# A decode block on one core: W2's four loads written behind the fills of the zero tiles instead of ahead of them

## The chip, the core and the metric

The kernel runs on one core of a Trainium2 chip. The metric is the device time of one execution in microseconds; less is better. The core has five engines, each with an instruction stream of its own: TensorE (PE in the profile, its weight loads PEld), VectorE (DVE), ScalarE (ACT), GpSimd (POOL) and SyncE (SP). A transfer is issued by an instruction on one of them and runs on 16 DMA engines.

## The reference

One decode step for two sequences (B = 2, one token each, D = 512) in float32: attention over a cache of 8192 positions with 32 heads of 128, then a channel MLP of width 1792, each with a residual around it.

```
x = A_x
h = x + _A_ref(_layernorm(x), K, V, wq, wo)        # attention
h2 = h + _B_ref(_layernorm(h), w1, b1, w2, b2)     # MLP

_A_ref: q = x @ wq; p = softmax(q K^T * Dh**-0.5); o = p V; return o @ wo
_B_ref: y = layernorm(x); g = gelu(y @ w1 + b1);   return g @ w2 + b2
```

The work is nearly all loading: 562.06 MB are read from HBM, most of it K and V.

## The kernel before

Heads go in pairs, 16 pairs by 2 sequences: 32 units, each with one K tile and one V tile of 128 partitions by 16384 numbers. VectorE multiplies K by q and sums up the scores, with GpSimd adding halves of three chunks in four. ScalarE makes the exponentials. TensorE sums over V in `values(i, t)`: 32 steps u of 512 columns each, in the profile two records a step. Nearly all loads are issued from GpSimd's queue by `soft` (line 437).

All large tiles share one ring of three buffers (`kv` in the profile; `slot()` gives out the oldest). The last to be given out are these. `vlast` is the V tile of the last unit, 31, loaded in four parts of 64, 32, 24 and 8 positions. `wt` holds W1, W2 and the biases, in the buffer that the weights Wo had before. `late` has the buffer of the V tile of unit 30, and `cut()` slices it from column 0 on into the small tiles of the program's end: `zeros` (columns 0 to 95, filled with zero at L700; `otz` and `lane` are its parts, and L703 copies ones into `lane`), then `wlc`, `base` and `basec`, then `wb` (columns 2144 to 2399, filled with zero at L722).

The order on each engine is the order of the code. `Waits` looks at every instruction as it is written and has it wait, by semaphores, for the latest instruction that still uses the same partitions and columns: a fill of `late` waits for those of TensorE's matmuls in `values(30)` that read the columns it covers. GpSimd's loads have semaphores of their own in turn (`soft_0` to `soft_11`).

TensorE's end is in this order: `values` of unit 30; the four parts of the last unit's `values`, with two matmuls of zeros (`keep_warm(FILL[0])`, which read `wb`) written between the second and third part, at u = 24; products with `lane`; `head_sum`; products with `otz`; W1 in two halves, each behind one of W1's two loads; W2 in 14 steps t, behind W2's four loads of 7, 4, 2 and 1 steps. `keep_warm` stands at four other places in between. At L793 VectorE adds the bias, and SyncE stores the result.

```
vlast = load(v, NU - 1, [(0, NS2 // 2), (NS2 // 2, 32), (NS2 // 2 + 32, 24), (NS2 - 8, 8)])
wt = slot()
...
late = slot()
...
zeros = cut(P, (TH + 1) * 32)
nc.gpsimd.memset(zeros, 0.0)
...
        if i == NU - 1 and u == 24:
            keep_warm(FILL[0])
```

Of the kernel before, what the change touches and what calls it, by code (L numbers as in the profile page):

```python
# [273 lines left out]
def tile_decode_block(nc, waits, x, k, v, wq, wo, wog, wol, w1, bias, w2, out):  # L274
    B, H, SK, DH = k.shape
    D = wq.shape[0]
    F = w1.shape[1]
    DC = D // P
    FN = F // NG
    FT = F // P  # L280
# [17 lines left out]
    def slot():  # L298
        return kv.tile([P, ROW], F32, name="kv", tag="kv")
# [136 lines left out]
    def soft(to, of, joined=True):  # L436
        nc.gpsimd.dma_start(to, of, single_packet=joined)  # L437
# [74 lines left out]
    def inverse(g):  # L512
        r = work.tile(list(RL[g].shape), F32, name="rl" if g < GL else "rlp")
        nc.vector.reciprocal(r, RL[g])  # L514
        RL[g] = r
# [159 lines left out]
    wt = slot()  # L675
# [5 lines left out]
    w1v = w1.rearrange("(p c) f -> p c f", c=DC)  # L681
    for c in range(0, DC, 2):
        soft(w1t[:, c:c + 2], w1v[:, c:c + 2])
    w2t = wt[:, DC * F:2 * DC * F].rearrange("p (t d) -> p t d", t=FT)
    w2v = w2.rearrange("(p t) d -> p t d", t=FT)
    for t, n in ((0, 7), (7, 4), (11, 2), (13, 1)):
        soft(w2t[:, t:t + n, :], w2v[:, t:t + n, :])

    inverse(GL)
    nc.scalar.activation(junk[:, 0:1], lt4[:, 0:1], AF.Sqrt)  # L690

# [3 lines left out]
    def cut(parts, n):  # L695
        at[0] += n
        return late[:parts, at[0] - n:at[0]]
# [22 lines left out]
    nc.vector.tensor_scalar(basec, base, bmean, None, op0=ALU.subtract)  # L720
    wb = cut(P, D // 2).bitcast(BF16)
    nc.gpsimd.memset(wb, 0.0)  # L722

    po2 = psq.tile([P, P], F32, name="po2", tag="qps")
    wp = psq.tile([P, D], F32, name="wp", tag="qps", ahead=1)
# [119 lines left out]
```

## Time and profile before

| | us |
|---|---|
| median of 3 runs | 1306.67 (1305.98 to 1308.36) |
| profiled execution | 1308.55 |
| its span | 1306.3 |
| PE busy | 383.8 (29%) |
| DVE busy | 951.4 (73%) |
| ACT busy | 51.7 (4%) |
| POOL busy | 484.0 (37%) |
| DMA, share of the chain of waits | 71% |

The span runs from the first to the last instruction of the profiled execution; its time has 2.25 us more around it. The transfers run at 430 GB/s over the span, with the DMA engines busy in nearly every slice, so the middle of the program is set by loading; the program's end is a chain of small dependent steps behind the last loads. Times in the views are from the span's start. L437 is the line of all loads from GpSimd, so they are told apart by their tensor and size; `in_w_dram` stands for W1 and W2 both. L194 is the helper's line for matmuls outside the loop.

### The profile page before, as it was taken

The page shows a single profiled execution, that of the slowest core. Times are in us where ns is not written, and L with a number is a line of the kernel's source. Part 1 is how long each engine was busy: PE and PEld are TensorE (multiplying, and loading weights), DVE is VectorE, ACT ScalarE, POOL GpSimd, SP SyncE. Part 2 cuts the span into 40 slices and gives each one's busy share as a digit, 9 for nine tenths or more (in the row PEclk, how much of TensorE's full clock was granted, in tenths as well). Part 3 has the DMA queues.
Part 4 walks back from the last instruction along what each step waited for, and adds up shares of the span by engine and source line. Part 5 has one row for each costly group of instructions (what it writes and reads, how often), then busy time and mean ns, then how long its engine had stood idle before and what let it go on. Part 6 is the DMA issues. An engine that isn't in the chain of part 4 may idle for free.

```text
span 1306.3 us, 6773 instructions
## 1 busy us (share of the span) xinstructions
PE 383.8 (29%) x2897; PEld 120.4 (9%) x2900; DVE 951.4 (73%) x411; ACT 51.7 (4%) x172; POOL 484.0 (37%) x215
## 2 busy tenths in 40 slices
PE   4005023230412323043331403333041332403267
PEld 1001000000100001010000101000010100101113
DVE  1988677779777778877778877777986777887742
ACT  0010000000000000000000000000000000000011
POOL 2444433244443234443234443324444323444320
PEclk9557566665666657566665756666566665656678
DMA  9999999999999999999999999999999999999997
GB/s 401 434 448 421 441 426 438 429 436 431 435 432 435 431 437 429 438 429 437 429 437 429 437 429 437 429 437 429 437 428 439 427 439 427 439 428 437 419 429 324
DMA packets 11500, 561.20 MB, mean 430 GB/s; under 512 B 1420, under 2 KB 1428, under 8 KB 1758
## 3 DMA queue, kind: packets, MB, share of 16 engines
q0 software_dynamic: 11168, 552.61, 97.9%
q1 hardware_dynamic: 314, 8.41, 1.6%
q8 instruction: 8, 0.13, 0.0%
q14 instruction: 6, 0.05, 0.0%
q10 hardware_dynamic: 4, 0.00, 0.0%
HBM read 562.06 MB, written 0.00 MB: 430 GB/s over the span
## 4 chain that ended last, share of the span: by engine, by line
DMA 71%; DVE 14%; POOL 11%; PE 2%; issue 2%; ACT 0%; DVEq 0%
DMA kv<-in_k_dram 69%; DVE kv L471 12%; POOL kv L475 10%; DVE s L478 2%; DMA kv<-in_wq_dram 1%; PE so L194 1%; PE qps L194 1%; POOL kv L437 0%; PE sm L194 0%; PE rowacc L194 0%; DVE rl L514 0%; DVE q L407 0%; ACT kv L784 0%; POOL kv L678 0%; POOL kv L722 0%
## 5 line engine op out<-in xcount | busy, mean ns | idle before, releaser
L471 DVE TENSOR_TENSOR kv<-kv,qps 128x4096 f32<-128x4096 f32 x128 | 564.0, 4407 | 277.0 <-DMA kv<-in_k_dram 275.0
L475 POOL TENSOR_TENSOR kv<-kv 128x2048 f32<-128x2048 f32 x96 | 434.1, 4523 | 472.3 <-DVE kv L471 272.0
L478 DVE TENSOR_REDUCE s<-kv 128x32 f32<-128x2048 f32 (+1 forms) x128 | 357.1, 2810 | 0.6 <-POOL kv L475 0.3
L242 PE MATMUL so<-kv,pt 128*16 128x512 f32 x1920 | 272.1, 730 | 270.8 <-DMA kv<-in_v_dram 248.6
L242 PE MATMUL sm<-ident,mx 128*1 128x128 f32 x30 | 9.7, 324 | 571.9 <-DVE mx L485 571.9
L437 POOL DMA_DIRECT2D kv<-in_v_dram x35 | 19.3, 551 | 273.0 <-DVE mx L485 251.7
L242 PEld LDWEIGHTS so<-kv,pt 128*16 128x16 f32 x1920 | 62.0, 112 | 456.0 <-DMA kv<-in_v_dram 250.0
L242 PEld LDWEIGHTS sm<-ident,mx 128*1 128x1 f32 x30 | 2.4, 79 | 578.0 <-DVE mx L485 574.9
L534 ACT ACTIVATE ss<-so 128x512 f32<-128x512 f32 x16 | 9.6, 597 | 551.3 <-PE so L242 514.1
L497 ACT ACTIVATE nb<-sm 128x4 f32<-128x4 f32 x16 | 2.8, 173 | 652.5 <-PE sm L242 649.5
L502 ACT ACTIVATE pt<-s,nb 64x128 f32<-64x128 f32 x64 | 25.5, 399 | 1.7
L437 POOL DMA_DIRECT2D kv<-in_k_dram x33 | 18.8, 570 | 8.7 <-DVE s L478 8.7
L194 PE MATMUL qps<-kv,pt 128*16 128x512 f32 x128 | 17.7, 702 | 8.7 <-DMA kv<-in_v_dram 8.7
L242 PE MATMUL sm<-ss,sel 128*4 128x128 f32 x120 | 15.6, 273 | 12.5 <-ACT ss L534 11.6
L407 DVE COPY q<-so 128x512 f32<-128x512 f32 x1 | 0.7, 691 | 18.3 <-PE so L194 18.3
L514 DVE RECIPROCAL rlp<-sm 128x4 f32<-128x4 f32 x1 | 0.2, 181 | 17.3 <-PE sm L194 17.3
L194 PE MATMUL so<-kv,yT 128*4 128x512 f32 x64 | 10.0, 793 | 8.6 <-DMA kv<-in_wq_dram 8.6
L490 DVE TENSOR_REDUCE gm<-sm 1x4 f32<-1x256 f32 x16 | 6.6, 412 | 7.3 <-PE sm L242 7.0
L242 PEld LDWEIGHTS sm<-ss,sel 128*4 128x4 f32 x120 | 9.3, 87 | 28.2 <-ACT ss L534 17.3
L502 ACT ACTIVATION_READ_ACCUMULATOR pt<-s,nb 64x1 f32 x64 | 11.8, 184 | 0.0
L437 POOL DMA_DIRECT2D kv<-in_w_dram x6 | 3.2, 534 | 22.9 <-issue 22.9
L242 PE MATMUL qps<-qs,pick 4*128 4x128 f32 x60 | 11.1, 306 | 0.0
(122 smaller groups left out, 160.4 us busy)
## 6 DMA issues: line engine op xcount, KB each, us to landing
kv<-in_k_dram POOLq DMA_DIRECT2D x2, 4096.0 KB, 18.3
kv<-in_wq_dram SPq DMA_DIRECT2D x1, 6656.0 KB, 18.3
kv<-in_wo_dram POOLq DMA_DIRECT2D x1, 6144.0 KB, 31.0
kv<-in_w_dram POOLq DMA_DIRECT2D x3, 1792.0 KB, 32.1
kv<-in_v_dram POOLq DMA_DIRECT2D x1, 4096.0 KB, 27.2
kv<-in_v_dram POOLq DMA_DIRECT2D x1, 2048.0 KB, 27.4
kv<-in_wq_dram SPq DMA_DIRECT2D x1, 1536.0 KB, 21.6
kv<-in_v_dram POOLq DMA_DIRECT2D x1, 1536.0 KB, 26.8
```

Source lines behind the costliest of these rows:

```text
L194: getattr(self.nc.tensor, what)(*aps, **how)
L242: ins = getattr(pe, what)(*aps, **how)
L407: nc.vector.tensor_copy(q2, so2[0])
L437: nc.gpsimd.dma_start(to, of, single_packet=joined)
L471: nc.vector.tensor_tensor(kc, kc, QP[g][:, b, None, :].to_broadcast([P, CH, DH]), op=ALU.mult)
L475: nc.gpsimd.tensor_tensor(kc[:, :, 0:HP], kc[:, :, 0:HP], kc[:, :, HP:DH], op=ALU.add)
L478: nc.vector.tensor_reduce(S[i][:, c * CH:(c + 1) * CH], chunk(t, c)[:, :, 0:n], axis=AX.X, op=ALU.add)
L490: nc.vector.tensor_reduce(gm, MT.pop(g).rearrange("o b (s p) -> o b s p", s=2), axis=AX.X, op=ALU.max, negate=True)
L497: nc.scalar.activation(nb, GM.pop(g), AF.Copy)
L502: nc.scalar.activation(ptz[b][q, :, 4 * m:4 * m + 4], s[q], AF.Exp, bias=nb[q, b, e:e + 1], scale=SCALE, accum_out=lt4[q, m:m + 1])
L514: nc.vector.reciprocal(r, RL[g])
L534: nc.scalar.activation(SS[g], so2[g == GL], AF.Copy)
```

## The change

The four loads of W2 are written some 30 lines later: behind the fill of `zeros`, the copy into `lane` and the fill of `wb`. Nothing is added or taken away, and all else stays in its place.

```
--- before.py
+++ after.py
@@ -681,11 +681,6 @@
     w1v = w1.rearrange("(p c) f -> p c f", c=DC)
     for c in range(0, DC, 2):
         soft(w1t[:, c:c + 2], w1v[:, c:c + 2])
-    w2t = wt[:, DC * F:2 * DC * F].rearrange("p (t d) -> p t d", t=FT)
-    w2v = w2.rearrange("(p t) d -> p t d", t=FT)
-    for t, n in ((0, 7), (7, 4), (11, 2), (13, 1)):
-        soft(w2t[:, t:t + n, :], w2v[:, t:t + n, :])
-
     inverse(GL)
     nc.scalar.activation(junk[:, 0:1], lt4[:, 0:1], AF.Sqrt)
 
@@ -720,6 +715,10 @@
     nc.vector.tensor_scalar(basec, base, bmean, None, op0=ALU.subtract)
     wb = cut(P, D // 2).bitcast(BF16)
     nc.gpsimd.memset(wb, 0.0)
+    w2t = wt[:, DC * F:2 * DC * F].rearrange("p (t d) -> p t d", t=FT)
+    w2v = w2.rearrange("(p t) d -> p t d", t=FT)
+    for t, n in ((0, 7), (7, 4), (11, 2), (13, 1)):
+        soft(w2t[:, t:t + n, :], w2v[:, t:t + n, :])
 
     po2 = psq.tile([P, P], F32, name="po2", tag="qps")
     wp = psq.tile([P, D], F32, name="wp", tag="qps", ahead=1)
```

GpSimd's last instructions, as a difference (`kv_0` is here `wt`, `kv_1` is `late`; "waits" names the semaphores that an instruction waits for):

```order
 L678 MEMSET kv_0 128x576 [waits by_PE]
 L437 DMA kv_0<-in_w1_dram 128x3584 x2
+L695 MEMSET kv_1 128x96 [waits by_PE]
+L698 COPY kv_1<-ident_0 2x2 [waits by_Pool]
+L717 MEMSET kv_1 128x512 [waits by_PE]
 L437 DMA kv_0<-in_w2_dram 128x3584
-L437 DMA kv_0<-in_w2_dram 128x2048 [waits by_soft_3]
+L437 DMA kv_0<-in_w2_dram 128x2048
 L437 DMA kv_0<-in_w2_dram 128x1024
 L437 DMA kv_0<-in_w2_dram 128x512
-L700 MEMSET kv_1 128x96 [waits by_PE]
-L703 COPY kv_1<-ident_0 2x2 [waits by_Pool]
-L722 MEMSET kv_1 128x512 [waits by_PE]
```

The two fills and the copy now stand ahead of W2's first load, with the waits that they had, and the order of the loads among themselves is the same. The second W2 load's own wait goes, as the fills' waits cover it.

TensorE's rows around the fill matmuls, the same before and after (`kv_2` is `vlast`, `kv_1` in the rows with `qps_2` is unit 30's V tile and in those with `qps_0` the tile `wb`):

```order
L194 MATMUL qps_2<-kv_1,pt0_0 16x512 [waits by_Activation,by_soft_7]
L194 MATMUL qps_2<-kv_1,pt0_0 16x512 x31
L194 MATMUL sm_0<-lt4_0,ones_0 128x4 [waits by_Activation]
L194 MATMUL qps_2<-kv_2,pt1_0 16x512 [waits by_soft_8]
L194 MATMUL qps_2<-kv_2,pt1_0 16x512 x15
L194 MATMUL qps_2<-kv_2,pt1_0 16x512 [waits by_soft_9]
L194 MATMUL qps_2<-kv_2,pt1_0 16x512 x7
L194 MATMUL qps_0<-kv_1 128x512 [waits by_Pool]
L194 MATMUL qps_0<-kv_1 128x512
L194 MATMUL qps_2<-kv_2,pt1_0 16x512 [waits by_soft_10]
L194 MATMUL qps_2<-kv_2,pt1_0 16x512 x5
L194 MATMUL qps_2<-kv_2,pt1_0 16x512 [waits by_soft_11]
```

Nothing moves on TensorE: the first fill matmul waits for GpSimd's fill of `wb` in both, ahead of the matmuls of V's third part (`soft_10`).

More of the change, by code (lines that the diff above doesn't have):

```diff
@@ L683, in tile_decode_block @@
         soft(w1t[:, c:c + 2], w1v[:, c:c + 2])
[L684 to L687, printed above, removed]
     inverse(GL)
@@ L722, in tile_decode_block @@
     nc.gpsimd.memset(wb, 0.0)
+    w2t = wt[:, DC * F:2 * DC * F].rearrange("p (t d) -> p t d", t=FT)
+    w2v = w2.rearrange("(p t) d -> p t d", t=FT)
+    for t, n in ((0, 7), (7, 4), (11, 2), (13, 1)):
+        soft(w2t[:, t:t + n, :], w2v[:, t:t + n, :])
     po2 = psq.tile([P, P], F32, name="po2", tag="qps")
```

## The prediction

> **What bounds the kernel now.** I read the chain of waits first, over the last 80 us, because the only instructions that change place belong to the end of the program. GpSimd's part of it (start, length, what):
>
> ```profile
> 1254.86 0.53 POOL kv L437
> ...
> 1255.41 0.54 POOL kv L437
> ...
> 1256.54 0.98 POOL kv L437 x2
> 1257.52 6.21 issue
> 1263.73 0.53 POOL kv L437
> 1264.26 9.13 issue
> 1273.39 0.53 POOL kv L437
> 1273.92 4.37 issue
> 1278.30 0.53 POOL kv L437
> 1278.83 3.19 issue
> 1282.01 0.54 POOL kv L437
> 1282.56 0.20 POOL kv L700
> ...
> 1282.98 0.47 POOL kv L722
> ...
> 1283.73 4.01 PE qps L194 x25
> ```
>
> The first two rows are the third and fourth parts of the last V tile, the x2 row is W1's two loads, and the four single L437 rows after it are W2's loads. Each of these four stands behind a stretch called "issue" (6.21, 9.13, 4.37 and 3.19 us): GpSimd holds the load in its hands and cannot give it out. Only after the fourth come the fills, L700 and L722, and only after L722 does TensorE go on. To see what TensorE was doing, I took the timeline of the same stretch (start, length, engine, line, operation, count; in brackets the idle time before it and its releaser):
>
> ```profile
> 1263.47 9.05 PE L194 MATMUL qps<-kv,pt 128*16 128x512 f32 x64 [7.11 <-DMA kv<-in_v_dram]
> ...
> 1273.13 3.63 PE L194 MATMUL qps<-kv,pt 128*16 128x512 f32 x32 [0.29 <-DMA kv<-in_v_dram]
> ...
> 1278.03 1.91 PE L194 MATMUL qps<-kv,pt 128*16 128x512 f32 x16 [1.28 <-DMA kv<-in_v_dram]
> ...
> 1283.73 0.38 PE L194 MATMUL qps<-kv 128*128 128x512 bf16 x1 [3.79 <-POOL kv L722]
> ...
> 1284.04 3.12 PE L194 MATMUL qps<-kv,pt 128*16 128x512 f32 x16
> ...
> 1287.28 0.60 ACT L534 ACTIVATE ss<-qps 128x512 f32<-128x512 f32 x1 [27.12 <-PE qps L194]
> ...
> 1294.07 2.07 PE L194 MATMUL so<-kv 128*32 128x448 f32 x16
> ...
> 1297.32 1.71 PE L194 MATMUL so<-kv 128*32 128x448 f32 x16
> ...
> 1300.93 3.27 PE L194 MATMUL qps<-kv 128*32 128x128 f32 x112 [0.28 <-DVE kv L787]
> ...
> 1304.31 0.29 DVE L793 TENSOR_TENSOR kv<-qps,kv 128x128 f32<-128x128 f32 x1 [3.03 <-PE qps L194]
> ```
>
> The x64 row is the values of unit 30; the next two are the first and second part of the last unit's values. Then TensorE sits idle for 3.79 us, released by the fill at L722, does its fill matmuls, and only then the third and fourth V parts (the x16 row at 1284.04). After that one dependent chain runs to the end: `gather` at 1287.28, W1 in two halves, W2, the last add. From 1287.28 to 1304.31 it is 17.03 us.
>
> GpSimd's "issue" times end with TensorE's: the second V part lets TensorE start at 1278.03, and 0.27 us later (1278.30) the next W2 load goes out; the first part does the same at 1273.13 and 1273.39, the V tile before at 1263.47 and 1263.73. So a load leaves when an older one has landed: with seven of them in flight the eighth waits. The zero tiles, which need no transfer at all, stand behind that.
>
> When the data was really there, the DMA issues tell (size, then us from issue to landing, a median where there are several; the bare line is that of W1's two loads alone, so the 32.1 between them is W2's first):
>
> ```profile
> kv<-in_w_dram POOLq DMA_DIRECT2D x3, 1792.0 KB, 32.1
> ...
> kv<-in_v_dram POOLq DMA_DIRECT2D x1, 1536.0 KB, 26.8
> kv<-in_w_dram POOLq DMA_DIRECT2D x1, 1024.0 KB, 25.0
> kv<-in_v_dram POOLq DMA_DIRECT2D x1, 512.0 KB, 27.5
> kv<-in_w_dram POOLq DMA_DIRECT2D x1, 512.0 KB, 21.3
> ...
> kv<-in_w_dram POOLq DMA_DIRECT2D x1, 256.0 KB, 18.2
> DMA to landing us min/median/max: 30.8/32.7/34.6
> ```
>
> V's third part landed at 1254.86 + 26.8 = 1281.66, its fourth at 1255.41 + 27.5 = 1282.91. TensorE started on the third at 1284.04. That is the time at stake.
>
> **The change part by part.**
>
> *What the fills wait for now.* In front of W2 they still wait for TensorE, since their buffer is that of unit 30's V tile. By the code the waits are by columns: the first fill covers columns 0 to 95, the other 2144 to 2399, so the last matmul in question is that of u = 4, the 9th and 10th of the 64 records at 1263.47. Its end isn't a row of its own. The earliest possible is 1263.47, the latest 1272.52 (all 64); twelve records have run by 1265.90 (the first clock row, below), so I take 1266.3. With 0.20, 0.18 and 0.51 us for fill, copy and fill they are done at about 1267.2, and at the latest at 1273.4. TensorE wants them at 1278.03 + 1.91 = 1279.94. Both ends are early enough.
>
> *What is queued behind that wait on GpSimd:* W2's four loads and nothing else. The first moves from 1263.73 to about 1267.2 (at worst 1273.4). The other three are released by landings at 1273.1, 1278.0 and 1281.7, which don't change, so they go out at 1273.39 (or 0.5 us behind the first), 1278.30 and 1282.01 as before. What hides the late first load is the queue: W1's second load lands at 1257.0 + 34.6 = 1291.6, and W2's first is behind it in any case, landing at 1263.73 + 32.1 = 1295.8. It has some 18 us to spare even at worst. Cost: nothing. Were that cover gone, every us would count. [...]
>
> *What goes.* TensorE does the two fill matmuls at 1279.94 and then waits for V's third part: 1281.66, seen at 1281.75 (0.26 us ahead of GpSimd's 1282.01, as above). The x16 group starts there and not at 1284.04: 2.29 us. This group took 3.12 us and the equal group at 1278.03 took 1.91. The reason is the granted clock (PEclk, the third figure from the right in the table by windows; the rows begin with the window, its length, and busy time and records of PE, PEld, DVE, ACT and POOL):
>
> ```profile
> 1263.40:1265.90 2.50, 2.43 (x12) 0.49 (x16) 0.00 (x0) 0.00 (x0) 0.53 (x1) 0.50 1.04 446
> 1267.00:1269.00 2.00, 2.00 (x24) 0.43 (x20) 0.00 (x0) 0.00 (x0) 0.00 (x0) 0.87 0.95 410
> 1278.00:1280.00 2.00, 1.91 (x16) 0.37 (x16) 0.00 (x0) 0.00 (x0) 0.53 (x1) 1.00 1.00 416
> 1284.50:1285.20 0.70, 0.70 (x9) 0.10 (x4) 0.00 (x0) 0.00 (x0) 0.00 (x0) 0.57 1.01 430
> 1288.00:1291.40 3.40, 3.40 (x19) 2.19 (x19) 0.17 (x1) 0.00 (x0) 0.00 (x0) 0.50 1.01 430
> 1294.00:1296.00 2.00, 2.00 (x24) 0.62 (x26) 0.00 (x0) 0.00 (x0) 0.00 (x0) 0.79 0.97 403
> ```
>
> It was 1.00 up to the long gap, fell to half within 1284.50 to 1285.20, and came back within 1294 to 1296. With the gap cut to about 1.4 us (1280.4 to 1281.75; the gap of 1.28 us before 1278.03 left the clock at 1.00), I expect it to hold through the values: 1.91 instead of 3.12 us, 1.21 us less. The fourth part's matmuls are needed at 1281.75 + 12/16 x 1.91 = 1283.18, after its landing at 1282.91. Values end at 1283.66 instead of 1287.16: 3.5 us in all, 2.3 if the clock falls anyway.
>
> *What is late next.* I leave the 17.03 us behind it at their length, half clock included. W1's second half would start at 1297.32 - 3.5 = 1293.8 (landed 1291.6), W2 at 1297.4 (1295.8), its second load's share, half way, at 1299.1 (1273.39 + 25.0 = 1298.4), the third's at 1300.0 (1278.30 + 21.3 = 1299.6), the last 8 of 112 records at 1300.5 (1282.01 + 18.2 = 1300.2). All transfers are just ahead. A faster chain gains nothing more: from 1300.2, 0.09 us to be seen, 8/112 x 3.27 = 0.23, about 0.3 for the last to end, and 0.1 to the add put it at 1300.9 against 1304.31. So the floor by W2's last load is a gain of 3.4 us, and that is what I take.
>
> *Sum.* The profiled execution took 1308.55 us (span 1306.3, and 2.25 around it), so 1305.15 after. It stands 1.88 us above the median of the three runs, 1306.67 (1305.98 to 1308.36). Taken off the median, 3.4 us give **1303.3**, 0.26%. About 0.2%, 2.6 us, is what a measurement of this kernel can tell from no change.
>
> **The rivals.**
>
> *The median had less to lose.* The three clock changes can be placed within their rows: 0.87 over 1267 to 1269, between 0.50 and 1.00, puts the rise at 1267.52 (74% of the 2 us at the full clock), 0.57 the fall at 1284.60, 0.79 the second rise at 1294.84. They lie 17.08 and 10.24 us apart, 5 and 3 times 3.415: the clock changes on a fixed grid, and where the grid falls against the gap may differ by execution. Had it fallen so that the clock came back a step or two earlier, TensorE's small matmuls between 1288 and 1294 would have run at twice the speed. The spread of the runs fits that: 1308.55 and 1308.36 on one side, 1306.67 and 1305.98 on the other. Then the median is an execution whose end was 1.88 us shorter already, and since the floor by W2's last load holds for both, only 3.4 - 1.88 = 1.5 us are left: 1305.2, 0.12%, within what can be told. Against it: the runs may differ by their 1250 us of loads as well. [...]
>
> *The clock stays at half to the end.* The fill matmuls at 1283.73 kept TensorE busy right ahead of the last values; they now run 1.8 us earlier, and TensorE, ahead of its data, meets new gaps before W1 and W2. If it is at half clock from the values through W2, the group of 1.91 takes 3.8 (+0.7 on 3.12), W1's halves 3.4 each (+1.35 and +1.71), W2 6.5 (+3.27): +7.0 against the 2.3 us won at the start, so 4.7 slower, 1311.4. It decides when the clock is not back by W1's first half. For it: it took 10.24 us to come back in the profile, busy as TensorE was. Against it: the same dense stretch that brought it back still comes, only earlier.
>
> *Nothing moves.* If the fills' wait ended later than 1281.7, the idle time would stay and the time be 1306.7. It would take a wait on the last unit's own matmuls, and the buffers differ, so this is unlikely.
>
> **How the numbers follow.** The forecast, 3.4 us less, has 0.60. The grid rival (1305.2) has 0.27 and "nothing moves" 0.04, both within 0.2%: 0.31. Half clock to the end has 0.09. The range goes from 1303.3 less half the runs' spread (2.38 / 2 = 1.2), 1302.1, to the grid rival plus nearly the same, 1306.3. It leaves out the last two cases, 0.13, and takes in a clock that falls during the values (2.3 us: 1304.4).
>
> **What would show it.** In the changed profile the fills stand at about 1266 to 1267.5, W2's first load right behind them and the other three at 1273.4, 1278.3 and 1282.0; TensorE's idle time ahead of the third V part ends with in_v_dram and not with a fill; the x16 group takes about 1.9 us; the add starts 3.4 us earlier, with W2's last load landing just before the last matmuls. I am wrong if W2's loads land later than 1300.2 (counted from an equal start), if the clock is at 0.50 during W2, or if the earlier end of the values is eaten by waits for in_w_dram.

## The result and the profile after

The changed kernel takes 1303.87 us (median of 17 runs, 1303.71 to 1305.28), the kernel before 1307.32 in 17 runs beside it (1303.81 to 1308.70, and one of 1326.36). That one is a slow execution, and the ratio leaves it out. The ratio is 0.9979, with a 95% interval of 0.9971 to 0.9987: faster by 0.21%, some 2.8 us. The profiled execution took 1303.98 us with a span of 1302.6. It has 1.38 us around its span where the profiled execution before had 2.25, so of the 4.57 us between the two, 3.7 are the program's.

GpSimd's last instructions in the changed kernel (timeline: start, length, engine, line, operation, count, and in brackets the idle time and its releaser):

```profile
1265.22 0.18 POOL L695 MEMSET kv<- 128x96 f32 x1 [7.73 <-PE qps L194]
1265.46 0.18 POOL L698 COPY kv<-ident 2x2 f32<-2x2 f32 x1
1266.87 0.53 POOL L717 MEMSET kv<- 128x512 bf16 x1 [1.23 <-PE qps L194]
1267.34 0.53 POOL L437 DMA_DIRECT2D kv<-in_w_dram  x1
1273.18 0.53 POOL L437 DMA_DIRECT2D kv<-in_w_dram  x1 [5.31 <-issue]
1278.08 0.53 POOL L437 DMA_DIRECT2D kv<-in_w_dram  x1 [4.37 <-issue]
1281.79 0.54 POOL L437 DMA_DIRECT2D kv<-in_w_dram  x1 [3.19 <-issue]
```

The fills are done by 1267.4 instead of 1283.4. W2's first load goes out 3.6 us later than before, the other three where they were. TensorE in the same execution (timeline of PE alone) and the last add:

```profile
1277.81 1.91 PE L194 MATMUL qps<-kv,pt 128*16 128x512 f32 x16 [1.27 <-DMA kv<-in_v_dram]
1279.88 0.38 PE L194 MATMUL qps<-kv 128*128 128x512 bf16 x1 [0.16 <-issue]
1281.53 2.31 PE L194 MATMUL qps<-kv,pt 128*16 128x512 f32 x16 [1.27 <-DMA kv<-in_v_dram]
...
1291.38 1.71 PE L194 MATMUL so<-kv 128*32 128x448 f32 x16 [0.19 <-DMA kv<-in_w_dram]
...
1295.67 1.74 PE L194 MATMUL qps<-kv 128*32 128x128 f32 x56 [0.97 <-DMA kv<-in_w_dram]
1298.18 1.08 PE L194 MATMUL qps<-kv 128*32 128x128 f32 x32 [0.77 <-DMA kv<-in_w_dram]
1299.44 1.05 PE L194 MATMUL qps<-kv 128*32 128x128 f32 x24 [0.18 <-DMA kv<-in_w_dram]
...
1300.64 0.29 DVE L792 TENSOR_TENSOR kv<-qps,kv 128x128 f32<-128x128 f32 x1 [5.31 <-PE qps L194]
```

The idle time ahead of the third V part is now 1.27 us and ends with its transfer, no longer with a fill. The group behind it took 2.31 us and not 1.91, because the weight loads of its last four records waited for V's fourth part (timeline of the weight loads):

```profile
1282.79 0.12 PEld L194 LDWEIGHTS qps<-kv,pt 128*16 128x16 f32 x4 [0.29 <-DMA kv<-in_v_dram]
```

From W1's second half on, TensorE waits for a load at every step (0.19, 0.97, 0.77, 0.18 us). W2 ran in one go before; now it is cut in three by its loads. The chain of waits says the same (start, length, what):

```profile
1278.08 21.32 DMA kv<-in_w_dram
1299.40 0.04 issue
1299.44 1.18 PE qps L194 x24
```

The load in the first row is W2's third, issued at 1278.08. The last 8 of the 24 records wait once more, for the fourth:

```profile
1300.07 0.16 PEld L194 LDWEIGHTS qps<-kv 128*32 128x32 f32 x8 [0.25 <-DMA kv<-in_w_dram]
```

And the granted clock (third figure from the right in the table by windows) stays whole where it was 0.50 before:

```profile
1284.00:1286.00 2.00, 2.00 (x27) 1.24 (x19) 0.17 (x1) 0.50 (x1) 0.00 (x0) 1.00 1.01 430
1288.00:1290.00 2.00, 2.00 (x34) 0.80 (x36) 0.48 (x2) 0.00 (x0) 0.00 (x0) 1.00 1.01 430
```

### The profile page after: what moved, and what is told of

Its sections match the earlier page's. It is cut to its first block, busy times and chain, and to the rows that moved or that the text cites. A ratio compares the mean times of both kernels' runs of the same rounds, so it can differ in the third digit from the quotient of the medians.

```text
span 1302.6 us, 6773 instructions
## 1 busy us (share of the span) xinstructions
PE 384.1 (29%) x2897; PEld 120.7 (9%) x2900; DVE 951.5 (73%) x411; ACT 51.7 (4%) x172; POOL 484.1 (37%) x215
## 4 chain that ended last, share of the span: by engine, by line
DMA 73%; DVE 14%; POOL 10%; PE 1%; issue 1%
DMA kv<-in_k_dram 67%; DVE kv L471 12%; POOL kv L475 10%; DMA kv<-in_v_dram 3%; DVE s L478 2%; DMA kv<-in_w_dram 2%; DMA kv<-in_wq_dram 1%; PE so L194 1%; PE qps L194 0%; PE rowacc L194 0%; POOL kv L455 0%; DVE rl L514 0%; POOL kv L437 0%; DVE q L407 0%; POOL kv L717 0%
## 5 line engine op out<-in xcount | busy, mean ns | idle before, releaser
L242 PE MATMUL so<-kv,pt 128*16 128x512 f32 x1920 | 276.5, 740 | 265.9 <-DMA kv<-in_v_dram 243.8
L242 PE MATMUL sm<-gm,srow 1*128 1x4 f32 x30 | 8.7, 359 | 7.6 <-DVE gm L490 7.6
```

The lines of the kernel that those rows point to most:

```text
L242: ins = getattr(pe, what)(*aps, **how)
```

## The experiments

The kernel before gave medians of 1305.13, 1305.65 and 1304.83 us in the three sets of runs below, since its single runs spread over more than 5 us (the last experiment is about that). Its lowest run is nearly the same in all of them: 1303.74, 1303.73 and 1303.86 us, and 1303.81 beside the changed kernel. Each kernel is therefore compared with the changed kernel's 1303.87 and by its own spread as well.

**Three of W2's loads ahead of the fills.** An edit of the kernel before:

```
-    for t, n in ((0, 7), (7, 4), (11, 2), (13, 1)):
+    for t, n in ((0, 7), (7, 4), (11, 2)):
         soft(w2t[:, t:t + n, :], w2v[:, t:t + n, :])
...
     nc.gpsimd.memset(wb, 0.0)
+    soft(w2t[:, 13:14, :], w2v[:, 13:14, :])
```

> Three of W2's four loads stand ahead of the fills as before, only the fourth (one step) behind. Theory A (TensorE's wait for the zero tile costs, and it is the fourth load alone that makes the fills later than TensorE's need at 1279.9): fills at about 1278.9 to 1279.8, so the time is that of the changed kernel, about 1303.9. Rival B (each load ahead of the fills costs its part): a quarter of the gain, about 1306.5. Rival C (what counts is W2's later place in the transfer queue): almost nothing is moved, so about 1307.

Measured: 1303.97 us (1303.69 to 1305.33, 11 runs), ratio 0.9986 (0.9976 to 0.9996). The timeline:

```profile
1278.35 0.53 POOL L437 DMA_DIRECT2D kv<-in_w_dram  x1 [4.37 <-issue]
...
1279.25 0.51 POOL L722 MEMSET kv<- 128x512 bf16 x1
...
1279.93 0.61 PE L194 MATMUL qps<-kv 128*128 128x512 bf16 x2
...
1281.80 2.29 PE L194 MATMUL qps<-kv,pt 128*16 128x512 f32 x16 [1.26 <-DMA kv<-in_v_dram]
```

The second fill ends at 1279.76, just ahead of TensorE at 1279.93. The spans of the 11 runs lie at 1302.4 to 1302.9, where those of the kernel before lie at 1302.4 to 1307.0. All of the gain is there with one load of 256 KB moved: theory A, and not a cost per load nor W2's place in the transfer queue.

**No fill matmuls at u = 24, loads as before.**

```
-FILL = (2, 3, 4, 3, 7)
+FILL = (0, 3, 4, 3, 7)
```

> The kernel before, with the two fill matmuls at u = 24 left out: all loads and fills keep their order, but TensorE has no wait for GpSimd in front of V's third part. Theory A: start on the third part at 1281.75, clock kept over a gap of 1.8 us, so the time of the changed kernel, 1303.9. Rival C (the order of the loads against the fills counts by itself): 1307, as before. Rival D (the two fill matmuls are needed to keep the clock): start early but the group at half clock, 1305 to 1306.

Measured: 1303.83 us (1303.73 to 1305.12, 11 runs), ratio 0.9989 (0.9980 to 0.9998). The fills stay at 1282.2 to 1283.1, the third V part starts at 1281.43 after 1.79 us of idle time, and the clock stays at 1.00. So neither the order of loads and fills nor the two matmuls count. What counts is TensorE's wait for GpSimd there, or what comes with it; the runs with a filled gap, below, part the two.

**The fills on VectorE, loads as before.**

```
-    nc.gpsimd.memset(zeros, 0.0)
+    nc.vector.memset(zeros, 0.0)
...
-    nc.gpsimd.tensor_copy(lane[:, 0:32:16], ident[:B, :B])
+    nc.vector.tensor_copy(lane[:, 0:32:16], ident[:B, :B])
...
-    nc.gpsimd.memset(wb, 0.0)
+    nc.vector.memset(wb, 0.0)
```

> The kernel before with the two fills and the copy on VectorE (behind its reciprocal, so at about 1273 to 1274), and W2's loads where they were on GpSimd. Theory A (only TensorE's wait for the zero tile counts): 1303.9. Rival C (the loads' place on GpSimd counts by itself): as the kernel before.

Measured: 1303.92 us (1303.82 to 1305.17, 12 runs), ratio 0.9986 (0.9977 to 0.9995). The fills stood at 1272.41 and 1276.97, the second later than I had expected but ahead of TensorE, which did its fill matmuls at 1279.59. This is a third way to the same time, with W2's loads where they were.

**W2's loads left out.** The changed kernel without its last loop over `soft`; the W2 product is taken with what lies in the buffer.

> The changed kernel without W2's four loads (its matmuls read what lies in the buffer; that part of the result is left out). Theory A (the changed kernel's end is set by W2's last load): W2's 112 records run in one go from about 1295.3, the last add stands near 1298.7 instead of 1300.64, about 1.9 us less than the changed kernel: 1302.0. Rival (the dependent chain sets the end): the same time as the changed kernel, 1303.9.

Measured: 1301.5 us (1301.4 to 1301.64, 6 runs). W2 runs in one go again, and the add stands at 1298.21:

```profile
1294.80 3.27 PE L194 MATMUL qps<-kv 128*32 128x128 f32 x112 [0.19 <-DVE kv L784]
...
1298.21 0.29 DVE L790 TENSOR_TENSOR kv<-qps,kv 128x128 f32<-128x128 f32 x1 [2.97 <-PE qps L194]
```

So in the changed kernel the dependent chain has 1300.64 - 1298.21 = 2.4 us to spare, and W2's last loads set the end. This was expected within 0.5 us.

**The gap filled, the wait left in.** To part the late start from the clock, matmuls of old data are put into the gap of the kernel before; nothing reads their result:

```
             if i == NU - 1 and u == 24:
+                for _ in range(13):
+                    pe.matmul(wp, ones, wlast[:, 0, :], start=True, stop=True)
                 keep_warm(FILL[0])
```

> The kernel before, with 13 matmuls of data that is long there (their result is never read) put into the gap ahead of the two fill matmuls that wait for GpSimd. The wait stays until about 1283.5, the granted clock should not fall. Theory A1 (most of the loss is the clock that falls in the gap): the third V part starts at 1284.0 as before but takes 1.9 us and not 3.1, the chain behind it runs at full clock, and the end comes within 0.5 us of the changed kernel: about 1304.2, and all runs close together. Theory A2 (the late start is the loss, the clock a detail): the 2.3 us of late start stay, about 1306.2.

Measured: 1311.0 us (1310.8 to 1311.2, 5 runs), ratio 1.0040 (1.0027 to 1.0054): neither theory, for I had sized the filling wrongly. Each matmul is two records of 0.44 us and not of 0.12, as those of the values are, so it overfilled the gap (11.43 us) and the third V part started at 1291.43. The run isn't without use: the last add came at 1307.66, 16.23 us after that start, with the groups as short as where the clock is at 1.00 (1.91 us for the 16 records of the third part, 1.71 for each of W1's halves, 3.26 for W2).

```profile
1279.64 11.43 PE L194 MATMUL qps<-wlast,ones 128*128 128x512 f32 x26
...
1291.43 1.91 PE L194 MATMUL qps<-kv,pt 128*16 128x512 f32 x16
...
1307.66 0.29 DVE L795 TENSOR_TENSOR kv<-qps,kv 128x128 f32<-128x128 f32 x1 [3.03 <-PE qps L194]
```

With 8 instead of 13:

> As gap_filled, with 8 matmuls in the gap where 13 took 11.4 us: 0.44 us for each of 16 records, about 3.5 us, so TensorE is free for the zero tile at about 1283.2 and the third V part starts near 1284.0, late as in the kernel before, at full clock. In gap_filled the stretch from that start to the last add took 16.2 us; from 1284.0 it would end at 1300.3, ahead of the end that W2's last load allows (1300.6). Theory A1 (the late start alone costs nothing, the loss is the clock): 1303.9 and a narrow spread. Theory A2 (the 2.3 us of late start are lost): 1306.

Measured: 1306.73 us (1306.53 to 1306.95, 12 runs), ratio 1.0007 (0.9998 to 1.0015). Missed again by the same mistake, since 16 records are 7.1 us and not 3.5; the start was at 1287.05 and the add at 1303.28, again 16.23 us, with the clock at 1.00 in every window of the table from 1269 on. Two points on one line: at full clock, a start after 1300.64 - 16.23 = 1284.41 should cost its lateness, and one before it nothing. The kernel before starts at 1284.04. With 4:

> As gap_filled, with 4 matmuls, 8 records of 0.44 us, about 3.5 us from 1279.6 to 1283.1, so TensorE waits for the zero tile as before (until about 1283.5) and starts the third V part at about 1284.0, at full clock. From start to last add it took 16.23 us in both earlier runs of this edit (1291.43 to 1307.66, 1287.05 to 1303.28), so 1284.0 gives 1300.2, ahead of the end set by W2's last load, 1300.6. Theory A1 (the late start alone costs nothing, all of the loss is the clock): 1303.9, narrow spread. Theory A2 (2.3 us of late start are lost): 1306.

Measured: 1303.88 us (1303.8 to 1304.3, 12 runs), ratio 0.9987 (0.9978 to 0.9996). TensorE's timeline of it:

```profile
1279.58 3.70 PE L194 MATMUL qps<-wlast,ones 128*128 128x512 f32 x8
1283.44 0.38 PE L194 MATMUL qps<-kv 128*128 128x512 bf16 x1 [0.16 <-issue]
1283.75 1.91 PE L194 MATMUL qps<-kv,pt 128*16 128x512 f32 x16
...
1296.60 2.61 PE L194 MATMUL qps<-kv 128*32 128x128 f32 x88 [0.28 <-DVE kv L789]
1299.36 1.05 PE L194 MATMUL qps<-kv 128*32 128x128 f32 x24 [0.15 <-DMA kv<-in_w_dram]
```

The third V part starts 2.2 us later than in the changed kernel, as in the kernel before, and the end is the same (the add at 1300.55). The clock is at 1.00 in every window from 1276 to 1302. So the late start by itself costs nothing, and a clock that doesn't fall is worth the whole gain. The profile before agrees: from the same start to the add it took 1304.31 - 1284.04 = 20.27 us, 4.04 more than the 16.23 at full clock. It had started 0.37 us ahead of 1284.41, and the other 3.67 us are the difference of the two adds (1304.31 and 1300.64; the landings of these executions differ by some 0.2 us). Beside a clock that falls the late start isn't free, though: it uses up most of the 2.4 us that would have taken up a part of the loss.

**A long gap that isn't GpSimd's.** The changed kernel with V's second and third part as one load:

```
-    vlast = load(v, NU - 1, [(0, NS2 // 2), (NS2 // 2, 32), (NS2 // 2 + 32, 24), (NS2 - 8, 8)])
+    vlast = load(v, NU - 1, [(0, NS2 // 2), (NS2 // 2, 56), (NS2 - 8, 8)])
```

> The changed kernel with V's second and third part loaded as one of 56 positions: TensorE has nothing to do from about 1276.6 to 1281.7, a gap of 5 us that has nothing to do with GpSimd, and then 28 records instead of 12. Theory A1 (a long gap drops the clock, and that is the loss): the 28 records and the chain behind run at half clock for a time; the end 2 to 5 us above the changed kernel, 1306 to 1309, as wide as the kernel before. Theory A2 (only lateness counts): 28 records at 0.12 us end the values at 1285.1, inside the slack of 2.6 us, so 1303.9.

Measured: 1305.35 us (1304.67 to 1306.4, 12 runs), ratio to the kernel before 0.9997 (0.9988 to 1.0006); 1.5 us above the changed kernel (1.1 us by the median of the spans), under what theory A1 named and well above A2's. The timeline and the table by windows:

```profile
1281.31 3.31 PE L194 MATMUL qps<-kv,pt 128*16 128x512 f32 x16 [4.85 <-DMA kv<-in_v_dram]
...
1285.33 1.91 PE L194 MATMUL qps<-kv,pt 128*16 128x512 f32 x16
```

```profile
1279.00:1282.00 3.00, 0.69 (x8) 0.32 (x12) 0.00 (x0) 0.00 (x0) 0.43 (x1) 0.95 0.99 412
1282.00:1285.00 3.00, 3.00 (x18) 0.32 (x6) 0.00 (x0) 0.00 (x0) 0.11 (x1) 0.50 1.04 440
1285.00:1288.00 3.00, 3.00 (x34) 0.74 (x32) 0.00 (x0) 0.60 (x1) 0.00 (x0) 0.99 0.97 411
```

After 4.85 us of idle time the first 16 records take 3.31 us and not 1.91. The clock fell at about 1281.7 and was back at about 1285.1, after one step, with TensorE in dense matmuls. That it costs less than I had expected fits that short fall.

**No fill matmuls at all** (the changed kernel with `FILL = (0, 0, 0, 0, 0)`).

> The changed kernel without any of the 19 fill matmuls. Theory A1: TensorE's pauses in the end are short (each under 2 us) until W1, so if the clock needs a long gap to fall, the time stays within 0.5 us of the changed kernel, 1303.9; if the sparse matmuls of head_sum count as a pause the clock falls and it is 1305 to 1308. The late-start theory A2: 1303.9 in either case, since nothing starts later.

Measured: 1303.99 us (1303.73 to 1304.59, 12 runs), ratio 0.9986 (0.9977 to 0.9995). The clock does fall, at about 1287.9, behind pauses of TensorE of only 0.26 and 0.61 us, and comes back soon. So theory A1's condition was wrong: a long gap isn't needed for a fall.

```profile
1286.03 1.10 PE L194 MATMUL sm<-kv 128*32 128x128 f32 x16 [0.26 <-DVE kv L550]
1287.74 3.12 PE L194 MATMUL so<-kv 128*32 128x448 f32 x16 [0.61 <-DVE kv L749]
```

```profile
1285.00:1288.00 3.00, 2.13 (x27) 1.32 (x31) 0.82 (x4) 0.00 (x0) 0.00 (x0) 0.98 1.03 435
1288.00:1291.00 3.00, 3.00 (x32) 1.25 (x28) 0.33 (x1) 0.00 (x0) 0.00 (x0) 0.50 0.98 416
1291.00:1294.00 3.00, 2.25 (x32) 0.78 (x24) 0.70 (x3) 1.81 (x4) 0.00 (x0) 0.95 1.03 438
```

W1's first half takes 3.12 us and not 1.71, but the 2.4 us to spare take it up. A fall of one step is hidden at this place; the three or four steps of the kernel before are not.

**The kernel before, profiled twice more.**

> The kernel before, unchanged, for a second profile. Theory G (a fixed grid on which the clock changes, falling differently against the gap in each execution): the late start is the same, third V part at about 2.3 us after its landing, but the clock falls and comes back at other times, and the span follows that: 1302.5 to 1307. If the clock's course is the same as in the first profile while the span is not, theory G is wrong and the loads make the spread.

> As before_again_1, a third profile of the kernel before: the same late start, and a span between 1302.5 and 1307 that goes with the clock's course over the last 25 us.

Measured: spans of 1305.9 and 1307.1 us. The third V part started 2.29 us (1281.36 to 1283.65) and 2.72 us (1281.54 to 1284.26) after TensorE could have had it (0.26 us ahead of W2's fourth load, as in the prediction), so the late start is nearly the same in all three. The clock isn't. In the second of the two new profiles (timeline, then the table by windows):

```profile
1277.82 1.91 PE L194 MATMUL qps<-kv,pt 128*16 128x512 f32 x16 [1.05 <-DMA kv<-in_v_dram]
...
1284.26 3.62 PE L194 MATMUL qps<-kv,pt 128*16 128x512 f32 x16
...
1305.13 0.29 DVE L793 TENSOR_TENSOR kv<-qps,kv 128x128 f32<-128x128 f32 x1 [3.03 <-PE qps L194]
```

```profile
1282.00:1284.00 2.00, 0.31 (x1) 0.13 (x2) 0.00 (x0) 0.00 (x0) 1.17 (x4) 0.53 1.05 446
...
1292.00:1294.00 2.00, 1.67 (x18) 0.89 (x20) 0.75 (x3) 0.00 (x0) 0.00 (x0) 0.50 0.99 419
1294.00:1296.00 2.00, 2.00 (x11) 0.40 (x12) 0.23 (x1) 0.00 (x0) 0.00 (x0) 0.56 0.95 395
```

It fell at 1282.1 and rose at 1295.8: 13.7 us, four steps of 3.415. In the first of the two the same reading gives 1284.4 and 1294.6, three steps, as in the profile that the prediction used:

```profile
1284.00:1286.00 2.00, 2.00 (x16) 0.31 (x8) 0.00 (x0) 0.00 (x0) 0.00 (x0) 0.59 1.03 437
...
1294.00:1296.00 2.00, 2.00 (x40) 0.84 (x32) 0.00 (x0) 0.00 (x0) 0.00 (x0) 0.85 0.97 405
```

The spans go with it: four steps 1307.1, three steps 1305.9 and 1306.3. From the third V part to the add it took 20.27 us in both executions with three steps (1283.65 to 1303.92 in the new one) and 20.87 in the one with four. Nor are the spans of the unprofiled runs spread evenly: in the 35 of the second set they lie at 1302.4 to 1302.6, 1303.3 to 1303.7, 1304.4 to 1304.5, 1305.8 to 1306.1 and 1306.9 to 1307.3. The lowest group is the changed kernel's span. That those runs have a clock that stays whole or falls for a step that the slack hides is argued and not shown, since none of them was profiled. Their mean clock over the whole execution is on record and doesn't settle it: 0.638 to 0.641 in the lowest group of all three sets, 0.636 to 0.638 in the highest, 0.631 to 0.637 in the one below that. The loads, the prediction's other suspect, can be ruled out for most of the spread: the changed kernel's end waits for them, and its 17 spans lie within 1302.4 to 1302.8. A part of the spread of the times isn't in the program at all, as the time stands 1.3 to 2.9 us above the span.

## Why the prediction was right, and where it wasn't

The sum said 1303.3, and 1303.87 came, inside the range and on the side forecast; the forecast of 3.4 us off the median stands against 2.8 us by the ratio. The wait that goes and the floor that stops the gain were right; what the wait costs was not.

*The fills' wait* was read rightly: by column, with fills done at 1267.2 by the estimate and 1267.4 measured, and the wait for u = 0 and u = 4 seen apart (7.73 and 1.23 us of idle time). The parts differ a little: u = 4 let the second fill go at 1266.87 and not 1266.3, but the first fill and the copy were done by then. With that, "nothing moves" fell.

*W2's later first load costs nothing*: right. It landed at 1267.3 + 28.3 = 1295.6 instead of 1295.8, and the others stayed. TensorE now waits 0.97 us for it, as its chain is earlier, but the end hangs on the last load.

*What goes* was wrong in its parts. I had 2.29 us for the late start and 1.21 us for the clock within the values, and left the 17.03 us behind them at their length, half clock included. With 4 matmuls in the gap the whole late start was still there, and the time was that of the changed kernel: the late start is worth nothing once the clock holds. The chain from gather to add is not 17.03 but 14.18 us at full clock (1293.48 to 1307.66 in the run with 13 matmuls); in the changed kernel it takes 16.73 (1283.91 to 1300.64) because it waits for loads. By itself the chain would have gained 6.1 us (1304.31 - 1298.21, the add without W2's loads) and not 3.5; that 3.5 came out next to the floor's 3.4 was luck. A smaller miss is V's fourth part: I had it landed before it was needed, but the group waited for it and took 2.31 us, 0.4 more than I said, which the 2.4 us to spare took up.

*What is late next* saved the number: the floor by W2's last load put the add at 1300.9, and it came at 1300.64, 3.67 us earlier than before. The run without W2's loads shows that it is a floor. The transfers were not "just ahead" of TensorE, as I had written, but behind it.

*The grid rival*, with 0.27, had the mechanism: in three profiles of the kernel before the steps of the clock fall differently (it falls at 1284.60, 1284.4 and 1282.1) and the span goes with it (1306.3, 1305.9 and 1307.1), and many of its runs have much less to lose, for the same reason as far as can be told without their profiles. Its evidence was weaker than it looked: of the 1.88 us that the profiled execution stood above the median, some 0.9 can be time around the span (2.25 us there, 1.3 to 1.4 in most runs). Its 1.5 us off the median isn't what the 17 runs beside the changed kernel gave (3.45 us between the medians), but in the later sets the kernel before had medians 1.0 to 1.8 us above 1303.87, close to it. That TensorE's small matmuls run at twice the speed at full clock holds only in part: the three groups from 1288 on took 1.87, 1.44 and 1.12 us in the profile before, at 0.50, and 1.06, 0.81 and 1.10 in the changed kernel's, at 1.00. How much is gained is a matter of the mix of runs, so that the measured gain lay near 3.4 and not near 1.5 is luck too. What the change does is to bring the runs to the lowest group: all 17 spans are there.

*The clock at half to the end* didn't come, in 17 runs no higher than 1305.28, and the run without fill matmuls shows that a fall of one step behind the values is taken up. The rival's lengths at half clock were near: the group of 1.91 us took 3.62 in the second new profile, and a W1 half of 1.71 took 3.12 without fill matmuls. But W2's 112 records took 3.26 or 3.27 us wherever they ran in one go, so half clock through W2 was not seen. That a dense stretch brings the clock back, as was argued against this rival, was my estimate: both rises in the first profile came in dense matmuls, but what brings them isn't shown.

## What to carry to other kernels

Where the chain behind it has time to spare, a wait of a few us on TensorE may cost nothing for its length and all of its price for the clock that falls with it (here a start 2.2 us late cost nothing at a clock of 1.00, and the add came 3.67 us later where the clock was at half for 10.24), so part the two: fill the gap with matmuls of no use, leave the wait, and see whether the time goes. Measure how far the chain may start late before the end moves, from a run that is late on purpose, instead of adding up waits. And where a queue makes an instruction wait for landings, as W2's loads did for 3.19 to 9.13 us each, small work that others need is best written ahead of the first load that is held up, or on another engine.

## What the runs showed of the hardware

In five executions the changes of the granted clock lay multiples of about 3.415 us apart (17.08 and 10.24 us in the first profile, 10.2 and 13.7 in the two others of the kernel before, 3.4 in the run with V's parts joined and in the one without fill matmuls), and where these steps lay differed by execution: the falls of the kernel before came at 1284.60, 1284.4 and 1282.1.

What makes the clock fall isn't settled by these runs. In the first profile TensorE was busy for 0.87 us of the 3.41 ahead of the fall at 1284.60, and in the second new one the clock fell at 1282.1, only 2.4 us after the last matmul had ended (1277.82 + 1.91 = 1279.73). Without any fill matmuls it fell behind pauses of 0.26 and 0.61 us, and without the two at u = 24 it held over one of 1.79 us. The profile's busy share doesn't tell whether the clock comes back either: in the first profile TensorE was busy in all of the 3.40 us behind the fall and stayed at half for another 6.8 us:

```profile
1281.19:1284.60 3.41, 0.87 (x9) 0.36 (x14) 0.00 (x0) 0.00 (x0) 1.37 (x4) 1.00 1.07 450
...
1284.60:1288.00 3.40, 3.40 (x32) 0.78 (x20) 0.00 (x0) 0.60 (x1) 0.00 (x0) 0.50 0.99 422
```

Matmuls of the same 128x512 columns took 0.44 us a record with 128 columns of weights (11.43 us for 26, in the gap filled with 13) and 0.12 us with 16 (1.91 us for 16), where four went to four quarters of the output in turn. I had taken the one for the other twice.
